# Turning the transformed SSM kernel with VectorE's 32x32 blocks instead of TensorE's transposes

## The chip, the cores and the metric

The kernel runs on one core of one Trainium2 chip. The metric is the device time of one execution, in microseconds (us), and the number shown is the median of several runs. Six things work side by side in a core: TensorE (PE in the profile, its weight loads PEld), VectorE (DVE), ScalarE (ACT), GpSimd (POOL), SyncE (SP, which here issues every transfer), and the 16 DMA engines that carry the transfers out. Each engine runs its own list of instructions in order and waits for others through semaphores.

## The reference

One block of a network: a modulated layer norm, a long causal convolution ("H3"), a gate, a second modulated layer norm and a SwiGLU feed-forward. All is float32, with 2048 positions, 512 channels and 1792 hidden units.

```python
mod = silu(c) @ w_mod                              # six vectors of 512: sa, ca, ga, sb, cb, gb
h  = layernorm(q) * (1 + ca) + sa
ks = sum_t k[s - t] * shift_k[:, t]                # 4 taps
kv = ks * v
y  = irfft(rfft(pad(kv)) * rfft(pad(ssm_k)))[:S] + kv * ssm_D
x  = q + ga * (h * y)
h2 = layernorm(x) * (1 + cb) + sb
out = x + gb * ((silu(h2 @ w_gate) * (h2 @ w_up)) @ w_down)
```

## The kernel before, in words

The kernel has two parts. The **front** makes `x`, normalizes it and forms the operands of the feed-forward. The **feed-forward** is a long row of 128x512 matmuls. It starts with the first product of the normalized input with gate and up weights (`gu_pe`, tile `g`).

**The convolution in the front.** The 512 channels are taken in four chunks of 128 (`c_` = 0 to 3). For each chunk the two sequences `kv` (called X) and `ssm_k` (called K) go through a two-step Fourier transform. They are multiplied point by point, and the product goes back through the inverse. For X the steps are:

- `tap0`, `tap`, `tms`, `tma`, `times_v`: the four taps and the product with v (ACT, DVE, POOL), with channels on the partitions.
- `x_turn`: TensorE transposes the chunk so that positions stand on the partitions (tile `kvt`), and ACT copies it out of PSUM.
- `x_first`: the first step of the transform, TensorE with the constant matrix `raw` (tile `er`) held and the data streamed. ACT copies the result (tile `s`) into `X[c_]`.
- `swap_x`: VectorE's transpose turns 32x32 blocks of `X[c_]` in place, four instructions for a chunk.
- `x3`: the second step (tile `px`, ACT copies it to `xs`), and `x_sum` (POOL or DVE) for the sum used by a three-multiplication complex product.

For K, before the change, the steps are:

- `k_first`: the first step, with the *data* (`SS[c_]`, tile `ss`) held and `raw` streamed. Channels then stand on the partitions. ACT copies the result in two halves into the tile `KT[c_]`.
- `k_turn`: TensorE transposes `KT[c_]`, 8 blocks of 128x128 at a time into one pair of PSUM banks (tile `kt`), and ACT (once DVE) copies the pair into `K[c_]`; four such steps for a chunk.

`KT` has one buffer for all four chunks (tag `f16`), and the last user of that buffer is the third piece of the modulation weights, `mod_load(2)`. Then `product3` forms the second step of K on TensorE (tile `pk`) and VectorE multiplies it with `xs`. `inv3` inverts the second step (tile `iv`), and ACT copies the result back into `X[c_]`. In `inv3s`, for the last chunk, VectorE turns it instead.

**Through memory and back.** Chunks 0, 1 and 2 then go out to device memory (`put`, one transfer of 2 MB, `away<-X`) and come back in another layout (`get`, four transfers of 512 KB, `X<-away`, pieces of 512 B). `y_pe` (tile `y`) is the last step of the inverse transform. It needs `X[c_]` back and the constant `einv` (tile `ei`). `y_into` and `y_gate` multiply `y` with the gate that `gate_n` (ACT) and `gate_p` (POOL or DVE) have made, and gather the statistics of the second layer norm. `rs1`, `rs2`, `rs3`, `norm1`, `norm_t`, `norm_s`, `hi1` and `lo1` make of them the first operands (`op`) of `gu_pe`.

**The order.** Nothing moves by itself: every instruction of an engine stands in program order, and the front is a list of calls written out by hand, one call a line. `e=act`, `e=dve` or `e=pool` says which engine does a step's vector work. A table `SLOTS` says which buffer each tile takes, so that a call may also wait for the last reader of a buffer. PSUM has four pairs of banks in the front (tag `ps`). SP issues all transfers in the order of the calls, and a transfer that must wait for a buffer holds up every transfer behind it.

## Time and profile before

| | |
|---|---|
| median of 3 runs | 574.13 us (574.13 to 574.15) |
| the profiled execution | 574.47 us, of which its span is 572.7 us |
| PE busy | 567.3 us, 99% of the span |
| DVE busy | 436.9 us, 76% |
| ACT busy | 301.0 us, 53% |
| POOL busy | 330.9 us, 58% |
| first `gu_pe` matmul | 152.09 us after the start of the span |
| granted TensorE clock | 1.00 |

The span runs from the first to the last instruction. The execution is 1.77 us longer than its span (574.47 - 572.7), and the profiled execution is 0.34 us above the median. Line 40 in the profile is the helper through which all engines record their instructions, so groups are told apart by their tiles: `kt<-ident,kt` are the transposes of `k_turn`, `kt<-s` the copies of `k_first`, `K<-kt` the copies of `k_turn`, `X<-X` the 32x32 turns of `swap_x`. A float32 matmul stands in the records as two instructions, a transpose as one.

### The profile page before, as it was taken

Reading aid. Unit: us, or ns where it says so; the run is one execution under the profiler, and the core shown is the slowest. Engines: PE = TensorE matmul, PEld = TensorE weight load, DVE = VectorE, ACT = ScalarE, POOL = GpSimd, SP = SyncE. Lnnn points to the kernel's source line nnn. Section 1 sums busy time; section 2 is a strip of 40 time slices with the busy share of each in tenths; the row PEclk is TensorE's granted clock in tenths of the full one; section 3 lists DMA queues with packets and bytes.
Section 4 is the critical chain, followed back from the end, with each engine's and each line's share of the span. In section 5 each row is a group of like instructions: output and inputs, shape, how many; then the busy total and the mean of one; then the engine's idle time right before and its main releaser. Section 6 shows DMA issues by size and latency. Waiting matters only on the chain.

```text
span 572.7 us, 10192 instructions
## 1 busy us (share of the span) xinstructions
PE 567.3 (99%) x4010; PEld 450.5 (79%) x4010; DVE 436.9 (76%) x625; ACT 301.0 (53%) x459; POOL 330.9 (58%) x303
## 2 busy tenths in 40 slices
PE   9999999999999999999999999999999999999997
PEld 9985476546888888888888888887888888888886
DVE  4897896989998866676576569857686868686766
ACT  3899989961754544434554556433434343434330
POOL 1348897789837866758979576452525252525210
PEclk9999999999999999999999999999999999999999
DMA  8976998997215364891899440354343434343403
GB/s 318 401 289 228 383 264 240 208 255 208 76 38 201 121 247 168 228 260 62 248 285 380 170 167 0 116 198 166 129 166 129 166 128 166 129 166 129 166 0 147
DMA packets 52545, 108.00 MB, mean 189 GB/s; under 512 B 19345, under 2 KB 34065, under 8 KB 46482
## 3 DMA queue, kind: packets, MB, share of 16 engines
q1 hardware_dynamic: 52498, 107.37, 55.9%
q8 instruction: 31, 0.51, 0.4%
q14 instruction: 16, 0.13, 0.1%
HBM read 72.74 MB, written 34.61 MB: 187 GB/s over the span
## 4 chain that ended last, share of the span: by engine, by line
PE 90%; DMA 3%; ACT 2%; DVE 2%; SPq 1%; issue 0%; POOL 0%; ACTq 0%; POOLq 0%
PE a L40 23%; PE dn L40 15%; PE c L40 12%; PE b L40 6%; PE da L40 6%; PE s L40 4%; PE g L40 4%; PE iv L40 3%; PE pk L40 3%; PE dc L40 3%; PE kvt L40 2%; DMA wm<-in_wmod 2%; PE kt L40 2%; PE px L40 2%; PE warm L40 1%; PE y L40 1%
## 5 line engine op out<-in xcount | busy, mean ns | idle before, releaser
L40 PE MATMUL a<-op,wsum 128*128 128x512 f32 x432 | 109.8, 390 | 0.0
L40 PEld LDWEIGHTS a<-op,wsum 128*128 128x128 f32 x432 | 81.0, 188 | 17.4 <-ACT p L40 0.4
L40 PE MATMUL dn<-wd,acts 128*128 128x512 f32 x336 | 84.8, 389 | 0.0
L40 PEld LDWEIGHTS dn<-wd,acts 128*128 128x128 f32 x336 | 63.1, 188 | 13.1
L40 ACT COPY p<-a 128x512 f32<-128x512 f32 x50 | 29.4, 587 | 57.7 <-PE a L40 57.7
L40 DVE TENSOR_TENSOR x<-x,dn 128x512 f32<-128x512 f32 (+1 forms) x65 | 43.2, 670 | 13.2 <-PE dn L40 12.9
L40 POOL TENSOR_TENSOR wa<-ws,wa 128x512 fp32r<-128x512 f32 (+1 forms) x28 | 32.0, 1165 | 26.2 <-ACT wa L40 26.2
L40 POOL TENSOR_TENSOR tb<-wds 128x256 f32<-128x256 f32 x12 | 8.9, 741 | 62.7 <-DVE wds L40 62.7
L40 ACT COPY r<-a 128x512 f32<-128x512 f32 x24 | 14.1, 587 | 53.8 <-PE a L40 53.8
L40 DVE TENSOR_TENSOR b<-r,c 128x512 f32<-128x512 f32 x24 | 16.7, 696 | 32.2 <-ACT sg L40 32.2
L40 POOL TENSOR_TENSOR wsum<-sr,wsum 128x512 fp32r<-128x512 f32 x28 | 40.1, 1456 | 0.0
L40 PE MATMUL c<-op,wsum 128*128 128x512 f32 x156 | 39.6, 389 | 0.0
L40 PE MATMUL c<-op,wa 128*128 128x512 f32 x156 | 39.6, 389 | 0.0
L40 PE MATMUL b<-op,wa 128*128 128x512 f32 x144 | 36.5, 389 | 0.0
L40 POOL TENSOR_TENSOR wd<-wds,wd 128x512 fp32r<-128x512 f32 x14 | 18.3, 1327 | 30.4 <-ACT wd L40 30.4
L40 PEld LDWEIGHTS c<-op,wa 128*128 128x128 f32 x156 | 29.3, 188 | 6.1
L40 PEld LDWEIGHTS c<-op,wsum 128*128 128x128 f32 x156 | 29.3, 188 | 6.1
L40 DVE TENSOR_TENSOR x<-x,da 128x512 f32<-128x512 f32 x48 | 32.7, 681 | 0.9 <-PE da L40 0.9
L40 DVE TENSOR_TENSOR xs<-pk,xs 128x1024 f32<-128x1024 f32 x24 | 27.6, 1213 | 7.3 <-PE pk L40 7.3
L40 PEld LDWEIGHTS b<-op,wa 128*128 128x128 f32 x144 | 27.0, 188 | 5.6
L40 POOL TENSOR_TENSOR s<-s,bcs 128x512 f32<-128x512 f32 x22 | 28.3, 1299 | 0.9
L40 ACT ACTIVATE sg<-a 128x512 f32<-128x512 f32 x26 | 15.5, 598 | 22.6 <-PE a L40 22.6
(200 smaller groups left out, 1352.2 us busy)
## 6 DMA issues: line engine op xcount, KB each, us to landing
ds<-wsum SPq DMA_DIRECT2D x12, 1024.0 KB, 7.6
wsum<-ds SPq DMA_DIRECT2D x12, 1024.0 KB, 6.4
dw<-wa SPq DMA_DIRECT2D x12, 768.0 KB, 5.9
wa<-dw SPq DMA_DIRECT2D x12, 768.0 KB, 4.3
ws<-in_wgu SPq DMA_DIRECT2D x16, 512.0 KB, 4.0
wds<-in_wdn SPq DMA_DIRECT2D x14, 512.0 KB, 4.8
...
```

The lines of the kernel that those rows point to most:

```text
L40: return lambda *a, **k: self.tc.keep_in_program_order(f(*a, **k))
```

## The change

K takes the way of X. `k_first` now holds `raw` and streams the data, so that its result has the layout of `x_first`'s and goes out of PSUM in one copy of 128x1024 for each step instead of two of 128x512. `k_turn` is gone. `k_swap` takes its place: four VectorE transposes in 32x32 blocks for each chunk, from `KT[c_]` into `K[c_]`. `x_first` is cut into four calls a chunk instead of two, with the same matmuls and copies. The list of the front is new throughout, and so are the buffer tables.

```diff
-    def x_first(c_, half, e=act):
-        if half == 0:
+    def x_first(c_, jq, e=act):
+        if c_ not in X:
             X[c_] = b16(f"X{c_}")
...
     def k_first(c_, jq, e=act):
         if c_ not in KT:
-            KT[c_] = f16(f"kt{c_}", (P, 4, 32, 32))
+            KT[c_] = f16(f"kt{c_}", (P, 32, P))
         ps = banks("s1")
         for jj in range(4):
             for a in range(2):
                 pe.matmul(
-                    ps[:, a, jj * P : (jj + 1) * P], SS[c_][rows(a), 4 * jq + jj], raw[rows(a), 4 * jq + jj],
+                    ps[:, a, jj * P : (jj + 1) * P], raw[rows(a), 4 * jq + jj], SS[c_][rows(a), 4 * jq + jj],
                     start=True, stop=True,
                 )
-        for a in range(2):
-            j = J * a + 4 * jq
-            copy(
-                e, KT[c_][:, :, j : j + 4, :].rearrange("p g j k -> p j g k"),
-                ps[:, a].rearrange("p (j g k) -> p j g k", j=4, g=4),
-            )
-
-    def k_turn(c_, m, e=act):
-        if m == 0:
+        copy(e, fours(KT[c_])[:, jq::4], ps.rearrange("p a (f d) -> p a d f", f=4))
+
+    def k_swap(c_, i):
+        if c_ not in K:
             K[c_] = b16(f"K{c_}")
-        ps = banks("kt").rearrange("p a (k d) -> p (a k) d", k=4)
-        src = KT[c_].rearrange("p g j k -> p (g j) k")
-        for k in range(8):
-            pe.transpose(ps[:, k], src[:, :, 8 * m + k], ident)
-        copy(e, fours(K[c_])[:, 2 * m : 2 * m + 2], ps.rearrange("p (g f) d -> p g d f", f=4))
+        r = slice(32 * i, 32 * i + 32)
+        dve.transpose(
+            fours(K[c_])[:, :, r].rearrange("p g d f -> p d g f"), fours(KT[c_])[:, :, r].rearrange("p g d f -> p d g f")
+        )
...
-    k_turn(3, 3, e=act)
...
+    product3(4, 0)
+    swap_x(14)
...
+    load_einv()
```

Several small steps change their engine in the new list. VectorE gives up one K copy, `mod_rep`, three `skip`, a `times_v`, an `x3` copy, `gate_n(2, 0)`, one of five `gate_p`, five of six `lo1`, two of four `add_y` and one of two `norm_s`. It takes one `x_first` copy and `wd_mul(0)`. POOL takes most of what VectorE gives up, and `mod_mul(0, 0)` from ACT. The feed-forward behind the front keeps its code.

VectorE's list at its start, from the first turns of chunk 0 to the products of chunk 0 (`K_308`, `K_320` are chunk 0's K, `u_300`, `u_296` the taps of chunk 2, `xs<-pk,xs` the products). Before:

```order
L40 STREAM_TRANSPOSE X_195<-X_195 128x32x8x4 x2
L40 COPY K_308<-kt 128x1024
L40 SCALAR_TENSOR_TENSOR u_300<-kt_245,sm,u_300 128x2047
L40 SCALAR_TENSOR_TENSOR u_300<-kt_245,sm,u_300 128x2046
L40 COPY crep<-csil 128x256
L40 SCALAR_TENSOR_TENSOR u_300<-kt_245,sm,u_300 128x2045
```

Now:

```order
L40 STREAM_TRANSPOSE X_196<-X_196 128x32x8x4 x4
L40 STREAM_TRANSPOSE K_320<-kt_248 128x32x8x4 x4
L40 SCALAR_TENSOR_TENSOR u_296<-kt_282,sm,u_296 128x2047
L40 SCALAR_TENSOR_TENSOR u_296<-kt_282,sm,u_296 128x2046
L40 SCALAR_TENSOR_TENSOR u_296<-kt_282,sm,u_296 128x2045
L40 TENSOR_TENSOR xs<-pk,xs 128x1024
```

All eight turns of chunk 0 now stand ahead of the taps of chunk 2, and the first product follows the taps at once.

SP's list from the first transfer out to memory to the last one back (`away` and `X<-away` are `put` and `get`, `x` the four loads of q, `ei` the constant for `y_pe`, `wm` modulation weights, `ws` gate and up weights). Before:

```order
L40 DMA x_718<-in_q 128x2048
L40 DMA ei<-in_e_inv 128x2048
L40 DMA away_786<-X_195 128x4096
L40 DMA x_788<-in_q 128x2048
L40 DMA x_790<-in_q 128x2048
L40 DMA X_195<-away_786 32x32x128 x4
L40 DMA away_1108<-X_400 128x4096
L40 DMA X_400<-away_1108 32x32x128 x4
L40 DMA ws<-in_wgu 128x1024
L40 DMA away_1498<-X_558 128x4096
L40 DMA wm<-in_wmod 128x2048
L40 DMA X_558<-away_1498 32x32x128 x4
```

Now:

```order
L40 DMA x_856<-in_q 128x2048
L40 DMA x_868<-in_q 128x2048
L40 DMA away_870<-X_196 128x4096
L40 DMA x_1091<-in_q 128x2048
L40 DMA X_196<-away_870 32x32x128 x4
L40 DMA away_1189<-X_410 128x4096
L40 DMA X_410<-away_1189 32x32x128 x4
L40 DMA ei<-in_e_inv 128x2048
L40 DMA away_1347<-X_547 128x4096
L40 DMA ws<-in_wgu 128x1024
L40 DMA wm<-in_wmod 128x2048 x2
L40 DMA X_547<-away_1347 32x32x128 x4
```

The constant `ei` has moved from ahead of the first `put` to behind the second `get`; two loads of q now stand ahead of the first `put`, and both halves of `wm` ahead of the last `get` instead of one on either side.

TensorE's list from the inverse of chunk 2 to that of chunk 3 (`y<-...` is `y_pe`). Before:

```order
L40 MATMUL iv<-xs,wc 64x512 x48
L40 MATMUL kt<-ident,kt_1293 128x128 x24
L40 MATMUL px<-X_1114,wc 32x512 x16
L40 MATMUL y<-X_195,ei 64x128 x8
L40 MATMUL y<-X_400,ei 64x128 x8
L40 MATMUL kt<-ident,kt_1293 128x128 x8
L40 MATMUL px<-X_1114,wc 32x512 x16
L40 MATMUL pk<-K_1475,wc 32x512 x48
```

Now:

```order
L40 MATMUL iv<-xs,wc 64x512 x48
L40 MATMUL px<-X_1024,wc 32x512 x8
L40 MATMUL y<-X_196,ei 64x128 x8
L40 MATMUL y<-X_410,ei 64x128 x8
L40 MATMUL px<-X_1024,wc 32x512 x8
L40 MATMUL warm<-ident 128x128 x5
L40 MATMUL px<-X_1024,wc 32x512 x16
L40 MATMUL pk<-K_1316,wc 32x512 x48
```

The transposes `kt` are gone, and the first `y_pe` stands ahead of three of the four `px` of chunk 3 instead of two.

More of the change, by code (lines that the diff above doesn't have):

```diff
@@ L282, in x_turn @@
         copy(e, x, pt)
[L284 to L287 removed]
+    def x_first(c_, jq, e=act):
+        if c_ not in X:
             X[c_] = b16(f"X{c_}")
[L289 to L304 removed]
+        x = XT[c_, jq // 2]
         ps = banks("s1")
@@ L1348, in adaln_h3_swiglu @@
-    product3(3, 2)
-    product3(3, 0)
-    product3(3, 1)
-    mod_mul(1, 1, e=act)
-    product3(2, 0)
-    product3(2, 2)
-    mod_part(1, 1, e=pool)
+    tap(3, 1)
+    product3(1, 2)
+    load_ssm(2)
+    x_sum(0, e=pool)
+    product3(0, 1)
+    tms(3, 2, e=act)
+    x_first(2, 0, e=act)
+    swap_x(7)
+    times_v(2, 2, e=pool)
+    x_first(2, 1, e=act)
+    product3(0, 0)
+    product3(0, 2)
+    mod_mul(0, 1, e=act)
+    swap_x(4)
+    k_swap(1, 0)
+    k_swap(1, 3)
+    k_swap(1, 1)
+    mod_part(0, 0, e=pool)
@@ new lines, in adaln_h3_swiglu @@
+    swap_x(5)
+    x_turn(2, 1, e=act)
+    tms(3, 3, e=act)
+    swap_x(6)
+    inv3(1, e=act)
+    tma(3, 2, 1, e=pool)
+    inv3(0, e=act)
+    x_first(2, 3, e=dve)
+    load_ssm(3)
+    k_swap(1, 2)
+    load_v(3)
+    x_first(2, 2, e=act)
+    swap_x(8)
+    swap_x(11)
+    swap_x(9)
+    do_stats(3, 0)
+    x3(2, 1, e=act)
+    tma(3, 2, 3, e=pool)
+    x3(3, 1, e=act)
+    x3(3, 2, e=act)
+    x_sum(3, e=dve)
+    product3(3, 0)
+    x3(2, 2, e=act)
+    skip(2, e=pool)
+    k_first(2, 0, e=act)
@@ new lines, in adaln_h3_swiglu @@
+    mod_part(0, 3, e=pool)
+    k_first(2, 1, e=act)
+    mod_mul(1, 0, e=act)
+    tma(3, 2, 2, e=pool)
+    x_sum(2, e=pool)
+    product3(2, 2)
+    room()
+    product3(3, 1)
+    product3(3, 2)
+    load_x(2)
+    product3(2, 0)
+    load_x(1)
+    put(0)
+    tma(3, 3, 2, e=pool)
+    x3(4, 2, e=act)
+    skip(3, e=pool)
+    tma(3, 3, 1, e=pool)
+    product3(2, 1)
+    times_v(3, 1, e=pool)
+    times_v(3, 3, e=pool)
+    times_v(3, 0, e=pool)
+    mod_mul(1, 1, e=act)
+    times_v(3, 2, e=pool)
@@ new lines, in adaln_h3_swiglu @@
+    inv3(3, e=act)
+    k_swap(2, 0)
+    inv3(2, e=act)
+    mod_part(1, 0, e=pool)
+    mod_part(1, 1, e=pool)
+    k_swap(2, 1)
+    mod_part(1, 2, e=pool)
+    k_swap(2, 2)
+    x_turn(3, 0, e=act)
+    mod_bc(0)
+    k_swap(2, 3)
+    x_turn(3, 1, e=act)
+    swap_x(10)
+    x3(4, 1, e=act)
+    mod_part(1, 3, e=pool)
+    k_first(3, 1, e=act)
+    x_first(3, 0, e=act)
+    x_first(3, 2, e=act)
+    x_sum(4, e=pool)
+    x_first(3, 1, e=act)
+    do_stats(1, 0)
+    mod_bc(1)
+    do_stats(3, 1)
@@ L1399, in adaln_h3_swiglu @@
+    gate_n(0, 1, e=act)
+    product3(5, 1)
+    load_einv()
     gate_p(0, 0, 1, e=pool)
-    load_w(1)
-    k_first(3, 3, e=act)
+    gate_p(0, 2, 1, e=pool)
+    product3(5, 2)
+    gate_n(2, 0, e=act)
     gate_n(3, 0, e=act)
-    swap_x(15)
-    swap_x(12)
-    gate_n(0, 1, e=act)
-    gate_p(0, 2, 1, e=pool)
+    inv3(4, e=act)
+    k_swap(3, 0)
+    k_swap(3, 3)
+    inv3(5, e=act)
+    put(2)
+    gate_p(3, 0, 1, e=dve)
+    x3(7, 1, e=act)
+    gate_p(0, 3, 1, e=pool)
+    y_pe(0, 0, 1)
@@ L1421, in adaln_h3_swiglu @@
[L1421 to L1442 removed]
+    y_into(0, 0, 1)
@@ L1452, in adaln_h3_swiglu @@
     inv3s(7)
     inv3s(6)
+    mod_row(2, 0)
+    mod_load(2, 1)
+    mod_row(2, 1)
     y_pe(2, 0, 1)
-    gate_p(2, 1, 1, e=pool)
-    gate_p(2, 3, 1, e=pool)
     y_gate(2, 0, 1)
-    y_pe(1, 0, 1)
-    gate_p(1, 2, 1, e=pool)
-    mod_row(2, 0)
+    mod_out(2, e=act)
+    get(2)
+    y_pe(0, 2)
+    y_pe(2, 2, 3)
+    y_into(0, 2)
+    y_pe(0, 3)
+    gate_p(1, 3, 1, e=pool)
     load_w(0)
-    y_pe(0, 3)
-    gate_p(3, 1, 1, e=pool)
+    w8_lo(1, e=pool)
     y_into(0, 3)
-    y_pe(0, 2)
@@ L1466, in adaln_h3_swiglu @@
-    mod_row(2, 1)
-    mod_out(2, e=act)
-    w8_lo(1, e=pool)
-    y_into(0, 2)
-    y_pe(2, 2, 3)
     rs1(0)
-    mod_T()
-    y_pe(1, 2, 3)
     rs2(0)
     rs3(0)
-    y_pe(3, 0, 1)
+    mod_T()
+    gate_p(1, 1, 1, e=dve)
+    y_gate(2, 2, 3)
+    load_wd(0)
     w8_hi(0)
```

440 lines of the change are left out of this document (178 added, 262 removed).

## The prediction

> **What bounds the kernel now.** I read the page first, then busy time by stretches, then the chain that ended last.
>
> ```profile
> span 572.7 us, 10192 instructions
> PE 567.3 (99%) x4010; PEld 450.5 (79%) x4010; DVE 436.9 (76%) x625; ACT 301.0 (53%) x459; POOL 330.9 (58%) x303
> ```
>
> TensorE is busy for 99% of the span, so work taken from it can shorten the kernel. The change touches only the front, which ends where the first feed-forward matmul `g` starts, at 152.09 us. Behind that point TensorE's work is unchanged, so I ask one thing only: by how much does `g` start earlier? I cut the front at the first data's arrival (4.86), at the end of chunk 2's products (107.62), at the end of the last turns (136.06), and at `g`:
>
> ```profile
> 4.86:107.62 102.76, 102.54 (x1486) 73.93 (x1490) 85.08 (x98) 91.96 (x123) 71.18 (x66) 1.00 0.91 301
> 107.62:136.06 28.44, 28.44 (x456) 15.73 (x440) 26.87 (x32) 15.54 (x18) 21.60 (x17) 1.00 0.92 244
> 136.06:152.09 16.03, 15.71 (x226) 13.54 (x218) 14.62 (x39) 8.94 (x12) 15.06 (x14) 1.00 0.36 113
> ```
>
> The columns are the length, then the busy time of PE, PEld, DVE, ACT and POOL, then the granted clock, the share of the DMA engines and GB/s. TensorE is full, but VectorE has only 17.7 us free in the first stretch (102.76 - 85.08) and 1.6 in the second. The transfers fill 0.91 and 0.92. Three resources lie close together, and the change lightens one of them. The chain shows how they meet at the end of the front:
>
> ```profile
> 104.86 5.35 PE iv L40 x88
> 110.23 1.94 ACT X L40 x2
> 112.19 6.98 DMA away<-X
> ...
> 126.34 12.29 DMA wm<-in_wmod
> ...
> 152.16 7.06 PE g L40 x30
> ```
>
> Chunk 2's inverse is copied out, goes to memory, comes back, and the last `wm` lands behind it at 138.63. So this end of the front hangs on two things: when chunk 2's products end, and what the transfers then need.
>
> **The change part by part.** *TensorE.* The removed transposes, and the two kinds of first-step matmul that change places:
>
> ```profile
> L40 PE MATMUL kt<-ident,kt 128*128 128x128 f32 x128 | 16.8, 282 | 0.2 <-ACT kt L40 0.2
> L40 PE MATMUL s<-x,er 64*128 64x128 f32 x256 | 15.9, 275 | 0.0
> L40 PE MATMUL s<-er,ss 64*128 64x128 f32 x256 | 15.7, 275 | 0.0
> ```
>
> On the chain 16 transposes take
>
> ```profile
> 37.73 1.99 PE kt L40 x16
> 83.64 1.80 PE kt L40 x16
> ```
>
> that is 0.113 to 0.124 us each, so 128 take 14.4 to 15.9; I take 15.9. Holding `raw` instead of the data costs nothing: X's matmuls of that form (15.9) take what K's took (15.7). TensorE's own floor for the kernel is thus 574.13 - 15.9 = 558.2. The Trainium skill (TensorE: Matmul & The Clock Gate, Part 4: PE-mode transpose) gives about 275 ns for such a transpose inside a kernel. By that the removal would be worth an estimated 128 x 0.275 = 35 us. The row's duration of 282 ns agrees with the page, but the chain shows that transposes overlap, so the duration isn't the price.
>
> *ScalarE and VectorE.*
>
> ```profile
> L40 ACT COPY K<-kt 128x1024 f32<-128x1024 f32 x15 | 15.7, 1094 | 0.7 <-PE kt L40 0.7
> L40 ACT COPY kt<-s 128x512 f32<-128x512 f32 x32 | 16.9, 691 | 0.3 <-PE s L40 0.2
> L40 ACT COPY X<-s 128x1024 f32<-128x1024 f32 x16 | 16.1, 1110 | 0.1
> L40 DVE STREAM_TRANSPOSE X<-X 128x1024 f32<-128x1024 f32 x16 | 19.1, 1218 | 1.5 <-ACT X L40 1.5
> L40 DVE STREAM_TRANSPOSE X<-iv 128x1024 f32<-128x1024 f32 x4 | 7.5, 2084 | 0.0
> L40 DVE COPY K<-kt 128x1024 f32<-128x1024 f32 x1 | 1.2, 1225 | 1.7 <-PE kt L40 1.7
> L40 DVE COPY xs<-px 128x1024 f32<-128x1024 f32 x1 | 1.2, 1225 | 2.3 <-PE px L40 2.3
> L40 DVE TENSOR_TENSOR ss<-ss,bcs 1x128 f32<-1x128 f32 x3 | 2.0, 651 | 0.0
> ```
>
> ScalarE loses 15.7 + 16.9 and gets back 16.1 for the 16 full copies. It gets 16.5 us lighter and bounds nothing. VectorE gets sixteen `k_swap`. One costs between 1.19 us (19.1/16, the turn of X) and 1.88 (7.5/4, the turn out of PSUM into another layout). The form is that of X's turn, from SBUF to SBUF with the same pattern, so I take 1.19: 19.1 us in all, up to 30.1 at the other end. Ahead of the end of chunk 2's products stand twelve of them (14.3 us) and one `x_first` copy (1.2). One turn of X (1.2) has moved behind that point. Gone are the two copies (2.4), the three `skip` (2.0), and two steps that the timeline shows:
>
> ```profile
> 38.62 0.74 DVE L40 TENSOR_TENSOR vt<-u,vt 128x512 f32<-128x512 f32 x1
> 94.09 0.99 DVE L40 TENSOR_SCALAR s<-x,rsa 128x512 f32<-128x512 f32 x2
> 100.74 6.88 DVE L40 TENSOR_TENSOR xs<-pk,xs 128x1024 f32<-128x1024 f32 x6 [3.38 <-PE pk L40]
> 139.76 0.68 DVE L40 TENSOR_TENSOR y<-y,s 128x512 f32<-128x512 f32 x1
> ```
>
> VectorE's work from 4.86 to the end of these products (now 100.74 + 6.88 = 107.62) becomes 85.1 + 14.3 + 1.2 - 1.2 - 2.4 - 2.0 - 0.7 - 1.0 = 93.3. Its floor for that point is 4.86 + 93.3 = 98.2, which is 9.4 earlier than now. TensorE's floor there, without the 96 transposes of chunks 0 to 2 (96 x 0.124 = 11.9 us), is 95.7. So **VectorE takes TensorE's place as the bound of the front**, and 9.4 is the most that it leaves. How much of the 9.4 comes depends on VectorE's remaining waits. Now it waits 17.7 us there, mostly for these:
>
> ```profile
> DVE xs L40 <- PE pk L40: 7.3, 3, 3.6
> DVE x L40 <- PE kvt L40: 2.5, 2, 1.6
> DVE xs L40 <- PE px L40: 2.3, 1, 2.3
> DVE K L40 <- PE kt L40: 1.7, 1, 1.7
> ```
>
> (total, times, longest). The waits of the two copies (2.3 and 1.7) go with them. The waits for `kvt` (2.5) and for the first data (1.0, the rest of the start) stay, since TensorE's first 15 us are the same. Of the other 10.2 us (7.3 of them for `pk`) I keep a quarter, 2.3, because TensorE now has 2.5 us less to do than VectorE up to that point (95.7 against 98.2). That gives 5.8 us of waits and an end of chunk 2's products at 104.0, which is 3.6 earlier. Both ends stay for the range: no waits but the start's 3.5 (101.7, 5.9 earlier) and all of today's but the copies' (111.9, 4.3 later).
>
> What the other engines take over has room. POOL is busy for 71.2 + 21.6 = 92.8 of the 131.2 us from 4.86 to 136.06. It gets some ten instructions more there, about 13 us at the 1.3 us of its commonest ones:
>
> ```profile
> L40 POOL TENSOR_TENSOR s<-s,bcs 128x512 f32<-128x512 f32 x22 | 28.3, 1299 | 0.9
> ```
>
> If that cover were gone, the first `y_into`, which waits for POOL's four `gate_p` of row block 0, would hold all products of chunk 3 behind it on VectorE.
>
> *The transfers behind chunk 2.* SP now sends `put(2)`, one `ws`, both `wm`, then `get(2)`. Plain loads ran at 388 GB/s, and the 512-byte pieces of `get` at about 210:
>
> ```profile
> 20.00:30.00 10.00, 9.78 (x115) 9.47 (x112) 8.26 (x7) 9.75 (x14) 5.91 (x5) 1.00 0.99 388
> 95.00:100.00 5.00, 5.00 (x96) 3.90 (x88) 2.36 (x3) 5.00 (x10) 2.85 (x4) 1.00 0.38 117
> 110.00:112.00 2.00, 2.00 (x23) 1.28 (x12) 1.97 (x3) 1.77 (x2) 0.48 (x1) 1.00 0.08 21
> 128.00:131.00 3.00, 3.00 (x60) 1.28 (x48) 3.00 (x3) 0.00 (x0) 2.85 (x3) 1.00 1.21 210
> ```
>
> `wm` needs the buffer of `KT`, which is free once the last `k_swap` has run. That is some 8 us behind chunk 2's products on VectorE, so before `put(2)` has landed, and the wait costs nothing unless VectorE is held up there. The sum: `put(2)` starts at 112.19 - 3.6 = 108.6, lands 6.98 later at 115.6, 0.5 + 2.1 MB at 388 take 6.8 (122.4), and the 2.1 MB of `get` at 210 take 10.0 (132.4). Now the chain has `wm` as the last to land; then it is `get(2)`, and three `y_pe` wait for it with 32 matmuls, two groups of this size:
>
> ```profile
> 136.38 1.97 PE L40 MATMUL y<-X,ei 128*64 128x128 f32 x32
> 152.09 7.13 PE L40 MATMUL g<-op,wg 128*128 128x512 f32 x30
> ```
>
> That is 3.9 us (136.3). From the last `y_into` of row block 0 (139.76) to `g` (152.09) it is 12.3 us now, through statistics, norm, transposes and splitting, the same steps as then. So `g` starts at 148.6, **3.5 us earlier**. The profiled execution would go from 574.47 to 571.0. It stands 0.34 above the median, so the median goes from 574.13 to **570.6**.
>
> **The rivals.**
>
> *VectorE and the transfers hide all but the start's waits.* For it speaks that nearly everything VectorE waits for comes from TensorE, which gets 15.9 us lighter. Against it speaks that the steps of one chunk depend on each other across three engines. With 2.0 us of waits chunk 2's products end at 100.2, 7.4 earlier. The same transfers and the same tail follow, and the time is 574.13 - 7.3 = 566.8. Even here TensorE's 15.9 are out of reach.
>
> *The waits stay as they are.* VectorE gets its turns, but waits 9 us or so in all, for PSUM pairs and for ScalarE's copies. Chunk 2's products then end near 107.6 and the time stays within 1.1 us of 574.1. For it speaks the order in which all eight turns of chunk 0 and three taps of chunk 2 stand on VectorE ahead of the first product, while TensorE's list has `pk` waiting for that product's PSUM pair.
>
> *The transfers come too late, and the kernel gets slower.* Two loads of q now stand ahead of the first `put`, one behind it, and `ei` behind the second `get`. So 4.2 MB of plain loads lie between vt's last load and `put(2)`, where 2.1 MB follow `put(0)` now. The other 2.1 MB cost 2.1/0.388 = 5.4 us. Free time of the DMA engines there is 3.1 us in 95 to 100 and 1.8 us in 110 to 112. The first is the turnaround between a `put` that lands and its `get`. SP's list has nothing to fill it with, since `ei` stands behind the `get`. Only 1.8 us are filled, and `put(2)` starts at 112.19 + 5.4 - 1.8 = 115.8 whatever VectorE has done. `ei` is late as well. The first `y_pe` waits for it on TensorE with three `px` and all `pk` of chunk 3 behind. With the same tail `g` starts 7.2 us later than forecast, at 155.8, and the time is 574.13 + 3.7 = 577.8. It decides from the point where chunk 1's `get` and `ei` land after 108.6; beyond 112.2 the kernel loses. Against it speaks that the three loads of q wait for buffers only, and may go early enough.
>
> *TensorE goes cold in its new waits.* The clock was 1.00 throughout, but TensorE also had no wait over 1.34 us. What a cold start costs, the first and second batch of `warm` show:
>
> ```profile
> 1.34 6.48 PE L40 MATMUL warm<-ident 128*128 128x128 f32 x32 [1.34 <-POOL ident masks.py:199]
> 23.12 1.38 PE L40 MATMUL warm<-ident 128*128 128x128 f32 x10
> ```
>
> 32 records would take 4.4 us at the second rate (0.138 each) and took 6.5, so 2.1 are lost. If the waits for `ei` and for `get(2)` each cause such a start, the forecast becomes 570.6 + 4.2 = 574.8, and a third one makes it 576.9, slower. The Trainium skill (TensorE: Matmul & The Clock Gate, Why this matters for your kernels) warns of idle gaps over about 3 us, behind which the array runs at half clock again. No run here shows such a gap yet.
>
> **How the numbers follow.** The forecast has 0.40, with its own range 568.1 to 572.9 (1.2 to 6 us faster). The fuller hiding has 0.20, no change 0.15, the late transfers 0.20, and three cold starts 0.05. The likeliest is the forecast: 570.6. For 8 times in 10 the range goes to 565.0 on the one side, beyond the second case's 566.8, and to 577.0 on the other, short of the third's 577.8, so that about 0.07 and 0.13 stay outside. A dearer `k_swap` (11 us on VectorE at 1.88) would also end beyond the upper end. Changes under 0.2% (1.15 us) can't be told from none: faster 0.40 + 0.20 = 0.60, same 0.15, slower 0.20 + 0.05 = 0.25.
>
> **What would show it.** TensorE's span share falls below 99%, by waits before `pk`, before the first `y` and before the `y` of chunk 2. `K<-kt` on VectorE has 16 rows near 1.19 us. VectorE is busy for over 90% from 4.86 to the end of the last turns, and chunk 2's products end near 104. `put(2)` starts near 108.6, the last thing to land ahead of `g` is `X<-away`, and `g` starts near 148.6. From `g` to the end it stays 420.6 us (572.7 - 152.1). The prediction is wrong if that last stretch grows (POOL late with the next weights), if `ei` lands after 108.6, if `k_swap` costs much over 1.2 us, or if the clock falls below 1.00.

## The result, and the profile after

The changed kernel takes 586.95 us (median of 4 runs, 586.70 to 587.41), against 574.14 us for the kernel before beside it. The ratio is 1.0223, with a 95% interval of 1.0205 to 1.0240: **slower by 12.8 us**. I had forecast 570.6.

The page of the changed kernel, to be read against the one before (span 572.7, PE 567.3 at 99%, clock full throughout):

```profile
span 584.9 us, 9904 instructions
PE 561.4 (96%) x3882; PEld 436.7 (75%) x3882; DVE 453.1 (77%) x624; ACT 286.9 (49%) x428; POOL 360.2 (62%) x319
PEclk9997999989998999999999999999999999999999
```

TensorE does 128 instructions less and is busy for only 5.9 us less. Its clock now dips twice in the front, and once behind `g` (175 to 190 us). POOL has 29.3 us more. Busy time by stretches, cut as in the prediction at the end of chunk 2's products, at the end of the last turns, and at `g`:

```profile
4.86:107.82 102.96, 95.13 (x1380) 60.70 (x1386) 94.38 (x101) 77.76 (x90) 84.26 (x73) 0.97 0.81 281
107.82:141.92 34.10, 28.00 (x440) 14.64 (x426) 28.40 (x30) 16.57 (x20) 25.28 (x20) 0.90 1.08 292
141.92:157.15 15.23, 14.22 (x214) 13.22 (x211) 14.92 (x37) 7.38 (x11) 13.95 (x12) 1.00 0.19 59
```

The first stretch is 102.96 us long, as long as before (102.76), with 7.4 us less of TensorE's busy time. The second grew from 28.44 to 34.10. So `g` starts at 157.15 instead of 152.09. From `g` to the first `dn` it is 26.5 us (157.15 to 183.61), against 21.0 before (152.09 to 173.09). That makes 5.06 + 5.46 of the 12.2 us of span. The other 1.7 lie right behind the first `dn`, as TensorE's rows show, in the changed kernel and in the one before:

```profile
183.61 2.54 PE L40 MATMUL dn<-wd,acts 128*128 128x512 f32 x6 [1.88 <-DVE wd L40]
173.09 1.52 PE L40 MATMUL dn<-wd,acts 128*128 128x512 f32 x6
```

TensorE waited 1.88 us ahead of it, and its granted clock was 0.58 from 183.61 to 186.15. These six took 1.02 us longer than before, and the twelve `g` behind them 0.73 (3.61 against 2.88). The chain that ended last, with columns start, length, engine, tile:

```profile
30.78 2.89 POOL wm L40
34.36 7.90 POOL wm L40 x3
42.25 2.04 POOL vt L40
...
89.79 12.29 DMA away<-X
103.97 11.83 DMA X<-away
115.80 2.44 issue
118.24 3.68 PE y L40 x32
...
134.41 7.04 DVE X L40 x4
...
164.19 2.35 DVE s L40 x2
166.54 4.46 DVE x L40 x2
```

Before, TensorE had 90% of this chain; now it has 75%. The chain passes through POOL's multiplication of `wm`, through `put(1)`, `get(1)` and another 2.44 us (in which, as the run with `ei` earlier will show, TensorE waits for `ei`) to the first `y`, and from 132 us up to `g` almost only through VectorE. TensorE's two longest waits stand in its own list (the bracket gives the idle time ahead of a group and what ended it):

```profile
45.38 2.33 PE L40 MATMUL kvt<-ident,vt 128*128 128x128 f32 x8 [4.78 <-POOL vt L40]
118.24 3.68 PE L40 MATMUL y<-X,ei 128*64 128x128 f32 x32 [6.10 <-issue]
```

### The profile page after: what moved, and what is told of

Read it like the earlier page. It is cut to its first block, busy times and chain, and to the rows that moved or that the text cites. A ratio compares the mean times of both kernels' runs of the same rounds, so it can differ in the third digit from the quotient of the medians.

```text
span 584.9 us, 9904 instructions
## 1 busy us (share of the span) xinstructions
PE 561.4 (96%) x3882; PEld 436.7 (75%) x3882; DVE 453.1 (77%) x624; ACT 286.9 (49%) x428; POOL 360.2 (62%) x319
## 4 chain that ended last, share of the span: by engine, by line
PE 75%; DVE 11%; DMA 4%; ACT 4%; POOL 3%; issue 2%; SPq 0%; DVEq 0%; ACTq 0%; POOLq 0%
PE a L40 22%; PE dn L40 15%; PE c L40 12%; PE b L40 6%; PE da L40 6%; PE dc L40 3%; PE pk L40 2%; DMA away<-X 2%; DMA X<-away 2%; POOL wm L40 2%; PE iv L40 2%; DVE x L40 2%; DVE X L40 2%; PE kvt L40 2%; DVE s L40 1%
## 5 line engine op out<-in xcount | busy, mean ns | idle before, releaser
L40 PEld LDWEIGHTS c<-op,wsum 128*128 128x128 f32 x156 | 29.3, 188 | 6.1
L40 PEld LDWEIGHTS c<-op,wa 128*128 128x128 f32 x156 | 29.3, 188 | 6.1
L40 POOL TENSOR_TENSOR s<-s,bcs 128x512 f32<-128x512 f32 x24 | 31.1, 1311 | 0.9
L40 PE MATMUL pk<-K,wc 64*32 64x512 f32 x384 | 25.1, 630 | 2.7 <-DVE xs L40 2.7
```

The source lines that it names most:

```text
L40: return lambda *a, **k: self.tc.keep_in_program_order(f(*a, **k))
```

## The experiments

Each time stands beside runs of the kernel before on the same chip. The runs of one kernel lie up to 3.6 us from their median, so I read differences between two variants from the intervals of their ratios.

### Order and turns apart

The change has two parts, so two orders with and without VectorE's turns give four kernels. The first run has the new `k_first` and `k_swap` in the old order, one `k_swap` at each of the 16 places of `k_turn`:

```diff
-            KT[c_] = f16(f"kt{c_}", (P, 4, 32, 32))
+            KT[c_] = f16(f"kt{c_}", (P, 32, P))
...
-    k_turn(0, 0, e=act)
-    k_turn(0, 1, e=dve)
+    k_swap(0, 2)
+    k_swap(0, 3)
```

> The order of the kernel before, with only the way K is transformed exchanged: the DFT matrix is stationary, and each of the 16 TensorE turns is replaced, at its place, by one VectorE turn. Theory O (the new order loses the time; turning K on VectorE costs no more than the 1.2 us per turn that was seen, and TensorE is relieved): 566 to 574 us, clearly below the changed kernel's 587. Rival V (VectorE as the bound of the front loses the time, whatever the order): 580 us or more.

It took 588.98 us, ratio 1.0259 (1.0233 to 1.0284). My theory fell at once: VectorE's turns alone, in the old order, cost as much as the whole change. The rows show where. VectorE's list in this run:

```profile
24.86 2.32 DVE L40 STREAM_TRANSPOSE K<-kt 128x1024 f32<-128x1024 f32 x2
...
37.91 2.37 DVE L40 STREAM_TRANSPOSE K<-kt 128x1024 f32<-128x1024 f32 x2 [3.30 <-ACT kt L40]
40.21 2.31 DVE L40 SCALAR_TENSOR_TENSOR u<-kt,sm,u 128x2045 f32<-128x2045 f32 x1
```

The last tap `u` of chunk 2 comes behind the turns: it starts at 40.21 and ends at 42.5, where before it ended at 35.2. Ahead of it stand six turns (7.05 us) and, in the second row, a wait of 3.30 us for ScalarE's copies of K. These copies waited in turn: at 32.29 ScalarE stood 2.27 us for VectorE's turns of chunk 0, because this order has one buffer for the copy (`KT`). So part of the cost here is that buffer's, not the turns'. POOL's `vt` waits for the tap, TensorE's `kvt` for `vt`. POOL and TensorE in this run:

```profile
42.65 5.07 POOL L40 TENSOR_TENSOR vt<-u,vt 128x512 f32<-128x512 f32 x3 [12.45 <-issue]
44.89 2.34 PE L40 MATMUL kvt<-ident,vt 128*128 128x128 f32 x8 [7.62 <-POOL vt L40]
123.99 0.34 SPq L40 DMA_DIRECT2D away<-X  x1
```

The third row is `put(2)` in SP's list, 11.8 us later than before (112.19). A single turn costs what I forecast; the price lies in what it delays on other engines.

The next run leaves all 16 turns out, so that only TensorE's and ScalarE's relief is left:

```diff
-            KT[c_] = f16(f"kt{c_}", (P, 32, P))
+            K[c_] = (f16 if c_ == 2 else b16)(f"K{c_}", (P, 32, P))
...
-    k_swap(0, 2)
-    k_swap(0, 3)
```

> The run with the old order and VectorE's turns (589 us), now without any turn of K: ScalarE copies the transformed K straight into the buffers that the products read, and the 16 VectorE turns are left out (so the products use K unturned, and the output is not the reference's). Theory V (VectorE's 16 turns, 18.9 us in its rows, are what costs; without them the removal of TensorE's 128 transposes is a gain): 558 to 570 us, chunk 2's products end at 98 to 104 instead of 118. Rival W (the time goes in the waits between the engines or in TensorE's slower clock behind them, and comes back whatever VectorE does): above 574, chunk 2's products end later than 107.6.

It took 572.40 us, ratio 0.9967 (0.9951 to 0.9983), a gain of 1.9 us by the ratio. Neither theory had that. Without any turn, the removal of 128 transposes and 32.6 us of ScalarE's copies, with 16 copies put in, is worth 1.9 us, not the 15.9 of TensorE's time. Its first stretch, up to the end of chunk 2's products:

```profile
4.86:106.40 101.54, 94.46 (x1392) 64.68 (x1394) 85.38 (x97) 82.57 (x97) 74.80 (x66) 0.97 0.91 303
```

It is 1.2 us shorter than before. TensorE is now idle for 7.1 us of it and VectorE, with as much work as before (85.4 against 85.1), still waits for 16.2. So most of the 17.7 us that I had read as VectorE waiting for a full TensorE don't come from TensorE's load. The run isn't a clean price of the relief, though. VectorE's taps started earlier, POOL's four `vt` beside them took 7.00 us instead of 4.99, and TensorE waited for them:

```profile
30.04 1.97 PE L40 MATMUL kvt<-ident,vt 128*128 128x128 f32 x8 [3.32 <-POOL vt L40]
```

Its granted clock was 0.50 from 30 to 34. So 1.9 us is what this order gains from the relief; that no other order would gain more isn't shown. The turns then cost (1.0259 - 0.9967) x 574.1 = 16.8 us in this order.

The new order without turns completes the four:

```diff
-            KT[c_] = f16(f"kt{c_}", (P, 32, P))
+            K[c_] = (f16 if c_ in (1, 3) else b16)(f"K{c_}", (P, 32, P))
...
-    k_swap(0, 0)
-    k_swap(0, 3)
```

> The changed kernel without any turn of K (ScalarE copies the transformed K straight into the buffers that the products read; the output is not the reference's). With the old order this took the time from 589 to 572. Theory V (the turns' 18.6 us on VectorE cost, in either order): 568 to 575. Rival O (the new order, with its work on POOL, its late loads and its tail, loses most of the time by itself): 578 or more.

It took 585.18 us, ratio 1.0187 (1.0157 to 1.0218). The rival holds. In the new order the turns cost (1.0223 - 1.0187) x 574.1 = 2.1 us, hardly more than the intervals leave open: the order hides them, or its own waits do. But the order by itself, with the engines that it gives the steps to, is (1.0187 - 0.9967) x 574.1 = 12.6 us slower than the old one, though both have the same work left out.

| | VectorE turns | no turns |
|---|---|---|
| old order | 589.0 | 572.4 |
| new order | 587.0 (the change) | 585.2 |

### What holds the time when TensorE is relieved

Two runs start from the old order without turns (572.4) and take POOL's adds of `wm` (six `mod_part`, twelve adds), or VectorE's statistics of q, out as well.

```diff
-    mod_part(0, 0, e=pool)
...
-    mod_part(0, 1, e=pool)
-    mod_part(0, 2, e=pool)
```

> The old order without turns of K (572.4 us), and POOL's twelve adds of wm left out in addition (15 us of POOL's work between 59 and 87 us; the output is not the reference's). The question is what holds this kernel at 572 when TensorE has lost 128 transposes and VectorE has no turn in their place. Theory Q (POOL's unbroken work from 51 to 104 us sets the pace): 564 to 569. Rival (VectorE or the transfers set it): 571 or more.

It took 570.32 us, ratio 0.9931 (0.9907 to 0.9955).

```diff
-        for i in rows_:
+        if name[0] == "a" and 0 in rows_:
+            dve.memset(mv, 1.0)
+        for i in rows_ if name[0] != "a" else ():
```

> The old order without turns of K (572.4 us), and VectorE's statistics of q left out in addition (16 pairs, 13.4 us of VectorE's work between 75 and 91 us, replaced by four memsets; the output is not the reference's). Theory V2 (VectorE set the pace of the front already in the kernel before, though TensorE was busy for 99%): 560 to 568. Rival (POOL or the transfers set it): 571 or more.

It took 570.77 us, ratio 0.9945 (0.9926 to 0.9964). The theories of a full POOL or a full VectorE asked for 3.4 and 4.4 us or more (569 and 568 us at most), their rivals for less than 1.4 (571 or more). The first got about 2; the second about 1, which the intervals hardly tell from nothing. Neither time lies clearly with one theory. `put(2)` moved from 110.91 to 106.81 and 108.52, `g` from 150.4 to 147.4 and 148.0. Taking 13 to 15 us from POOL or VectorE alone frees 2 to 3 us ahead of `g`. So none of the three engines TensorE, POOL and VectorE sets the pace alone. Transfers and ScalarE weren't tested in this way.

### The new order's waits, one at a time

The first run takes POOL's long multiplication away:

```diff
-    mod_mul(0, 0, e=pool)
+    mod_mul(0, 0, e=act)
```

> The changed kernel with the first four multiplications of wm by csil on ScalarE instead of POOL. Theory O1 (POOL's 11.5 us for them hold vt, and through it the transposes of chunk 2 on TensorE, which then sits idle for 4.8 us): that idle time goes, put(0) starts 3 to 5 us earlier and the time falls to 582 to 585. Rival (VectorE's own work is the bound there, and the idle time only moves): 586 to 588, and put(0) starts within 1 us of 72.2.

It took 586.21 us, ratio 1.0207 (1.0169 to 1.0245): not told from the change. `put(0)` did start 5 us earlier (67.12 instead of 72.15) and TensorE's wait for `kvt` went. What came in its place, in VectorE's, POOL's and TensorE's lists of this run:

```profile
65.65 6.75 DVE L40 TENSOR_TENSOR xs<-xs 128x512 f32<-128x512 f32 x2
67.29 1.27 POOL L40 TENSOR_TENSOR u<-u,tm 128x512 f32<-128x512 f32 x1
68.94 1.25 POOL L40 TENSOR_TENSOR u<-u,tm 128x512 f32<-128x512 f32 x1
70.27 5.73 POOL L40 TENSOR_TENSOR vt<-u,vt 128x512 f32<-128x512 f32 x4
73.79 3.50 PE L40 MATMUL pk<-K,wc 64*32 64x512 f32 x32 [5.27 <-DVE xs L40]
140.94 5.38 PE L40 MATMUL y<-X,ei 128*64 128x128 f32 x64 [4.22 <-issue]
```

Two adds of VectorE that take 0.7 us each when POOL is quiet took 6.75 here, the first 5.10 (65.65 to 70.75) and the second 1.74, beside a POOL that paused only at 70.2. TensorE waited 5.3 us behind them and then ran `pk` in 3.50 instead of 1.95. At the end, the `y` of chunk 2 waited for `get(2)`, which nothing had brought forward.

The second run loads `ei` earlier:

```diff
     put(1)
+    load_einv()
     get(1)
...
-    load_einv()
```

> The changed kernel with the load of ei issued between put(1) and get(1) instead of behind get(1). Theory O2 (the first y matmuls wait 6.1 us for ei, and px and pk of chunk 3 stand behind them): the wait goes, VectorE's last turns out of PSUM end 3 to 6 us earlier than 141.9, and the time falls to 581 to 584. Rival (these y matmuls would wait for X of chunk 1, which get(1) brings later still, or the stall moves to get(2)): 586 to 588.

It took 586.33 us, ratio 1.0218 (1.0171 to 1.0265). The wait for `ei` went, with 1.15 us for `get(1)` left in its place, and chunk 3's turns ended at 136.6, 5.3 earlier, as the theory said. But `g` started at 157.5. The rival had it: the stall moved to `get(2)`.

```profile
140.22 5.38 PE L40 MATMUL y<-X,ei 128*64 128x128 f32 x64 [4.16 <-issue]
```

The third run has the old end of the front, from the last inverse on, with those gates in it that the new order has still to do there. Three of the steps that moved, `...` marking what is left out between:

```diff
     inv3s(6)
...
+    gate_p(3, 2, 1, e=pool)
...
+    wd_mul(0, e=pool)
...
-    gate_p(3, 2, 1, e=dve)
...
-    add_y(2, 0, 4, (0, 1), e=pool)
...
-    wd_mul(0, e=dve)
...
+    add_y(2, 0, 4, (0, 1), e=dve)
```

> The changed kernel up to the last inverse transform, and from there the order and engines of the kernel before (gates of rows on POOL, sums of x and y on VectorE, subtractions of op mostly on VectorE, wd multiplied early on POOL). Theory O3 (POOL and VectorE hold each other up when both read two SBUF operands at once, and this costs the 5.4 us between the first g and the first dn): g to the first dn takes 21 to 22 us instead of 26.5, and the time falls to 581 to 583. Rival (the stretch is long only because its inputs come late from the front): it stays at 25 us or more, and the time at 585 to 588.

It took 588.17 us, ratio 1.0242 (1.0221 to 1.0263). TensorE's list:

```profile
158.31 0.47 PE L40 MATMUL nt<-ident,n 128*128 128x128 f32 x1 [5.54 <-ACT n L40]
166.89 7.10 PE L40 MATMUL g<-op,wg 128*128 128x512 f32 x30
187.83 1.52 PE L40 MATMUL dn<-wd,acts 128*128 128x512 f32 x6
```

From `g` to `dn` it took 20.9 us, as the theory said, and from `g` to the end 420.5, against 420.6 in the kernel before. But POOL still had 14 of its gate instructions to do (135.52 to 153.66) and came to the variance at 156.1; ScalarE's norm waited 10.0 us for it and TensorE 5.5. `g` started 9.7 us later. The wait moved to the other side of `g`.

### Two prices measured at the head

Ahead of the first data POOL and VectorE are idle, so extra instructions there show a price by itself. The times of these two kernels (590.59 and 609.54 us, one run each) aren't the question. The first of two runs asks what a multiplication by a column costs on POOL.

```diff
+    for _ in range(2):
+        pool.tensor_scalar(du[:, 0], du[:, 0], mhalf[:, 0:1], None, op0=ALU.mult)
+        pool.tensor_scalar(du[:, 0], du[:, 0], -0.5, None, op0=ALU.mult)
+        pool.tensor_tensor(du[:, 0], du[:, 0], du[:, 1], op=ALU.mult)
```

> The changed kernel with six extra POOL instructions at its head, on a buffer of their own, while POOL has nothing else to do until 11 us: multiplication of 128x512 by a column, by a constant, and by a second operand, once before VectorE's first work and once during VectorE's taps. Theory A (multiplying by a column is dear on POOL by itself): the first one takes 2.3 us or more with VectorE idle. Theory B (it is as cheap as the other forms, about 1.3 us, and took 2.9 because VectorE's taps held the way to SBUF): 0.7 to 1.4 us with VectorE idle, and over 2 only during the taps.

```profile
2.33 1.58 POOL L40 TENSOR_SCALAR du<-du,mhalf 128x512 f32<-128x512 f32 x1 [1.04 <-DVE du L40]
3.99 1.50 POOL L40 TENSOR_SCALAR du<-du 128x512 f32<-128x512 f32 x1
5.58 1.27 POOL L40 TENSOR_TENSOR du<-du 128x512 f32<-128x512 f32 x1
6.95 1.88 POOL L40 TENSOR_SCALAR du<-du,mhalf 128x512 f32<-128x512 f32 x1
```

It costs 1.58 us with VectorE idle and 1.88 beside VectorE's short taps, so neither theory is right. In its place in the changed kernel it took 11.49/4 = 2.87. There the four took 3.60, 2.71, 2.70 and 2.52 us, beside VectorE's long taps. Two of these taps took 2.66 us each, and 2.35 in the run with `wm` on ScalarE, so each slows the other. That the taps are the whole of the difference isn't shown.

The second sets VectorE and POOL against each other.

```diff
+    for _ in range(7):
+        dve.tensor_tensor(dd[:, 0], dd[:, 0], dd[:, 1], op=ALU.mult)
+    for _ in range(12):
+        pool.tensor_tensor(du[:, 1], du[:, 1], du[:, 1], op=ALU.mult)
+    for _ in range(6):
+        dve.transpose(dw, dv)
```

> The changed kernel with extra instructions at its head, ahead of the first data, on buffers of their own: four two-operand multiplications 128x512 on VectorE alone, three on POOL alone, then eight on VectorE and twelve on POOL at once, and six 128x1024 turns on VectorE while POOL's go on. Theory P (two-operand instructions of VectorE out of SBUF and POOL's can't run at once): VectorE's rise from 0.67 us to 1.3 to 2 us each, or wait for the whole of POOL's row; the turns, with one operand, stay at 1.2. Rival (the two run side by side): 0.67 and 1.27 us each throughout.

```profile
4.29 2.08 DVE L40 TENSOR_TENSOR dd<-dd 128x512 f32<-128x512 f32 x3
11.89 10.08 DVE L40 TENSOR_TENSOR dd<-dd 128x512 f32<-128x512 f32 x7
21.89 7.63 DVE L40 STREAM_TRANSPOSE dw<-dv 128x1024 f32<-128x1024 f32 x6
7.18 20.15 POOL L40 TENSOR_TENSOR du<-du 128x512 f32<-128x512 f32 x15 [5.89 <-DVE du L40]
```

Theory P holds. VectorE's multiplication takes 2.08/3 = 0.69 us alone and 10.08/7 = 1.44 beside POOL. POOL's row mixes cases: one instruction took 1.26 alone, 1.37 beside VectorE's multiplications and 1.04 beside the turns. The turns, with one operand, take 1.23 to 1.25 beside POOL. The Trainium skill (SBUF — State Buffer, Who interferes with whom) says that a VectorE instruction with two SBUF inputs contends with a GpSimd instruction that reads SBUF. The same page of the Trainium skill (Summary: rules for kernel authors) says that the second to issue is blocked until the first finishes. The trace agrees that they hold each other up. That each waits for the whole of the other it doesn't show: 1.44 us for one is less than 0.69 + 1.04. In the run with `wm` on ScalarE the add that took 5.10 us ran beside four POOL instructions that followed each other without a gap, and ended 0.5 us behind the first pause in POOL's list (0.08 us at 70.2). At the head POOL pauses as long between any two. That the add needs such a pause is inferred.

### Repairs together

Single repairs move waits. The next runs put them together. First `wm` and `ei`:

```diff
-    mod_mul(0, 0, e=pool)
+    mod_mul(0, 0, e=act)
...
     put(1)
+    load_einv()
...
-    load_einv()
```

> The changed kernel with two repairs at once: wm multiplied on ScalarE and ei loaded ahead of get(1). Each alone moved the time by under 1 us. Theory S (waits stand side by side: behind ei the next one is chunk 2's way through memory, which starts when VectorE has ended chunk 2's products, and neither repair touches that): g still starts within 1.5 us of 157.2 and the time is 584 to 587. Rival (the two repairs work on different stretches and add up): g at 153 or earlier and 581 or less.

It took 586.97 us, ratio 1.0227 (1.0199 to 1.0254), with `g` at 155.6, at the edge of theory S. The two don't add up to a gain in the time.

Then VectorE's sum of `xs` was moved to POOL, on top of the multiplication on ScalarE:

```diff
-    x_sum(3, e=dve)
+    x_sum(3, e=pool)
```

> The run with wm multiplied on ScalarE, and in addition the sum of xs for product 3 on POOL instead of VectorE, where its two adds took 6.75 us (65.65 to 72.40) instead of 1.4 while POOL ran without a gap. Theory P (VectorE's two-operand adds out of SBUF wait for POOL's instructions, which also read SBUF): VectorE loses the 5 us of waiting, TensorE's idle time of 5.3 us before pk goes, chunk 2's products end 3 to 5 us earlier than 107.3 and put(2) starts at 108 to 110; the time itself then falls by 1 to 4 us, to 582 to 585. Rival (the adds were waiting for their input from ScalarE, not for POOL): put(2) stays at 112 to 113 and the time at 586 or more.

It took 593.46 us, ratio 1.0332 (1.0313 to 1.0352), within the rival's range (586 or more), but with `put(2)` at 117.54, later than either theory had it. POOL's list is full there, and the sum came late:

```profile
  POOL xs L40: 13.4, 3
```

That is the idle time of VectorE ahead of the products, ended by POOL's `xs`. All repairs on top of this run did not mend that:

```diff
     put(1)
+    load_einv()
...
-    mod_load(2, 0)
     inv3s(7)
     inv3s(6)
-    mod_row(2, 0)
+    get(2)
+    mod_load(2, 0)
     mod_load(2, 1)
...
     lo1("B21", 1, e=pool)
+    wd_mul(0, e=pool)
...
-    add_y(2, 0, 4, (0, 1), e=pool)
+    add_y(2, 0, 4, (0, 1), e=dve)
     norm_s(1, 2, e=dve)
-    wd_mul(0, e=dve)
```

> All repairs together on the changed kernel: wm multiplied and the sum of xs moved as in the run above, ei loaded ahead of get(1), get(2) issued ahead of both wm loads (TensorE's rows for wm then behind the y of chunk 2), and at the end of the front one row gate moved from VectorE to POOL, the sums of x and y all on VectorE and wd multiplied on POOL. Theory (several waits stand side by side at the end of the front, chunk 3's products behind ei and chunk 2's way through memory, so that only removing all of them shows): g starts at 148 to 152, g to the first dn takes 21 to 24 us, and the time is 568 to 577. Rival (VectorE's total work in the front bounds it, and each repair only moves a wait): g at 156 or later and 583 or more.

It took 592.18 us, ratio 1.0309 (1.0290 to 1.0328). `put(2)` was at 117.2 already, so the run says nothing on the repairs behind it. The next run goes back to the one with `wm` and `ei`, has the same repairs at the end without the moved sum, and gives two gates to POOL in its idle time:

```diff
-    mod_load(2, 0)
     inv3s(7)
     inv3s(6)
-    mod_row(2, 0)
+    get(2)
+    mod_load(2, 0)
...
     w8_lo(1, e=pool)
+    gate_p(1, 1, 1, e=pool)
+    gate_p(3, 2, 1, e=pool)
...
-    gate_p(1, 1, 1, e=dve)
...
-    gate_p(3, 2, 1, e=dve)
+    wd_mul(0, e=pool)
...
-    add_y(2, 0, 4, (0, 1), e=pool)
+    add_y(2, 0, 4, (0, 1), e=dve)
```

> The run above, and in addition get(2) issued ahead of both wm loads, TensorE's rows for wm behind one y, two row gates moved from VectorE to POOL where POOL sits idle for 6 us, wd multiplied on POOL, and the sums of x and y all on VectorE. Theory S: with get(2) landing at 132 to 136 instead of 141, g starts at 149 to 153, g to the first dn takes 22 to 24 us, and the time is 573 to 579. Rival (VectorE or POOL are full up to g, and the wait moves again): g at 156 or later and 583 or more.

It took 582.84 us, ratio 1.0148 (1.0120 to 1.0176). That is faster than the change by (1.0223 - 1.0148) x 574.1 = 4.3 us. In the profiled execution the gain lies between `g` and `dn` (24.0 us instead of 26.5) and behind `dn`; `g` itself was at 158.5, as the rival had it. `get(2)` came earlier, but now the `wm` behind it was last, and TensorE's rows for `wm` stood ahead of `y`. From the chain:

```profile
128.98 11.20 DMA wm<-in_wmod
140.22 1.96 PE mr L40 x16
```

The transfers that follow chunk 2 end near 140 us in either order: with `wm` first `get(2)` was last, here `wm`. The next run lets VectorE's sum read one operand from PSUM:

```diff
-            e.tensor_tensor(t[:, a], xs[n, 1][:, a], xs[n, 2][:, a], op=ALU.add)
+            e.tensor_tensor(t[:, a], xs[n, 1][:, a], (xs[n, 2] if e is pool else xs[n, 2, "ps"])[:, a], op=ALU.add)
```

> The run above, and in addition VectorE's sum of xs for product 3 reads one of its two operands from PSUM instead of SBUF. Theory P (the 6.75 us of these two adds were waiting for POOL, which shares the way to SBUF with two-operand instructions of VectorE, as the run at the head showed with 1.44 us against 0.69): they take 1.4 us, TensorE's wait of 5.3 us before pk goes, put(2) starts 3 to 5 us earlier and the time falls by 2 to 5 us against the run above, to 569 to 576, which would be at or under the kernel before. Rival (their input from ScalarE was late, or VectorE's later work fills what they leave): put(2) within 1 us of the run above, and the same time.

```profile
65.57 1.25 DVE L40 TENSOR_TENSOR xs<-xs,px 128x512 f32<-128x512 f32 x2
162.76 6.81 DVE L40 TENSOR_TENSOR x<-x,s 128x1024 f32<-128x1024 f32 x3
```

The two adds took 1.25 us instead of 6.75, and `put(2)` started at 110.80, 3.1 earlier than in the run above: theory P on both counts, with the same POOL beside it. The time was 583.36 us, ratio 1.0156 (1.0137 to 1.0176), no better. Of 3.1 us at `put(2)` only 0.9 were left at `g` (157.6). Nor is the repair free: TensorE waited 3.09 us for the PSUM that the sum now holds, and 4.36 for `get(1)`. The last row shows the same contention behind `g`: three sums of x and y took 6.81 us, where before four took 5.3.

The last two runs mend TensorE's list at the two waits that this trace shows. The first of them also changed POOL's list:

```diff
-    y_pe(0, 0, 1)
     swap_x(12)
...
     x3(6, 1, e=act)
+    y_pe(0, 0, 1)
     k_swap(3, 2)
...
-    mod_row(2, 0)
-    mod_row(2, 1)
-    mod_out(2, e=act)
-    y_pe(0, 2)
...
     y_into(0, 3)
+    y_pe(0, 2)
...
+    mod_row(2, 0)
+    mod_row(2, 1)
...
     rs3(0)
+    w8_lo(1, e=pool)
+    gate_p(1, 1, 1, e=pool)
+    gate_p(3, 2, 1, e=pool)
```

> The run before (583 us), with TensorE's list mended at two places where that run's trace shows it waiting: the matmuls for wm stand behind the y of row block 0 instead of ahead of them (there they held y for wm until 138.8), and three px of chunk 3 stand ahead of the first y (which waited 4.4 us for get(1)); POOL's root of the variance is ahead of its last weights and gates. Theory S (TensorE's order of waiting is what is left): chunk 3's turns end 2 to 4 us earlier, g starts at 151 to 154 and the time is 576 to 580. Rival F (VectorE, POOL and the transfers are all full up to g, so that no order of TensorE gains): g at 156 or later, 582 to 585. In neither case does the kernel come under the 574 of the kernel before.

It took 586.62 us, ratio 1.0230 (1.0211 to 1.0249), with `g` at 160.7: later than both theories. POOL sat idle for 7.6 us ahead of the variance and then held VectorE's `y` of row block 1: a wait of my own making. Without that placement:

```diff
     load_w(0)
+    w8_lo(1, e=pool)
+    gate_p(1, 1, 1, e=pool)
+    gate_p(3, 2, 1, e=pool)
     y_into(0, 3)
...
     rs3(0)
-    w8_lo(1, e=pool)
-    gate_p(1, 1, 1, e=pool)
-    gate_p(3, 2, 1, e=pool)
```

> The run before (586.6 us), with POOL's last weights and two gates put back ahead of the root of the variance: behind it, they left POOL idle for 7.6 us and came late for y of row block 1 (VectorE waited 2.7 us, ScalarE's norm 2.7). Theory S: chunk 3's turns still end near 136.4, g starts at 152 to 156 and the time is 577 to 581. Rival F (all three resources are full up to g): g at 157 or later, 582 or more. In both cases it stays above the 574 of the kernel before.

It took 582.47 us, ratio 1.0143 (1.0126 to 1.0160). TensorE's waits went, chunk 3's turns ended at 136.3, and `g` started at 156.6, between the two expectations and nearer to the rival. VectorE then waited 2.0 us for `pm` and 2.3 for the next `y`. Together the repairs take 4.6 us of the 12.8 off. No version came under the kernel before, and none of the runs points to one that would.

## Why the prediction was wrong

**"TensorE is full, so work taken from it can shorten the kernel": this step failed first.** It read a busy share of 99% as the bound. The run without turns has all of TensorE's relief and nothing on VectorE in its place, and gains 1.9 us of 15.9, less than the 3.5 that I forecast with all the turns on VectorE. My quoted rows name only the last link of VectorE's waits, `pk` on TensorE. The runs' rows show what stands ahead of it: taps, `vt`, `kvt` and `xs`, in which TensorE is one link of several.

**"VectorE takes TensorE's place as the bound", floor 98.2, 5.8 us of waits: the work was right, the waits weren't.** VectorE's work up to the end of chunk 2's products is 94.38 us (forecast 93.3), and a turn costs what I took:

```profile
L40 DVE STREAM_TRANSPOSE K<-kt 128x1024 f32<-128x1024 f32 x16 | 18.6, 1206 | 0.0
```

But the waits are 102.96 - 94.38 = 8.6, so the products end at 107.82, not 104.0. The largest of them stands behind `kvt`, `vt` and POOL's `wm`:

```profile
49.70 1.23 DVE L40 TENSOR_TENSOR xs<-pk,xs 128x1024 f32<-128x1024 f32 x1 [5.49 <-PE pk L40]
```

This was the term on which the whole gain of 3.5 us rested. I had kept a quarter of the waits because TensorE has less to do (a quarter of 10.2 is 2.6, too, not the 2.3 that I added). As most of the waits weren't TensorE's, that had little ground. My rival of unchanged waits (within 1.1 us of 574.1) was nearer up to this point; the one in which the waits are hidden still better was further off.

**"POOL has room", ten more instructions at 1.3 us: mis-sized, and asked in the wrong way.** The four multiplications took 11.49 us, not 5.2. More than the price, it matters what was queued behind them: `vt`, with TensorE's `kvt` behind it (4.78 us idle). And POOL's load isn't free of VectorE's. A sum over busy shares can't see that the two hold each other up.

**`put(2)` to `get(2)`, 23.8 us: mis-sized.** `put(2)` started at 113.11, not 108.6. `get(2)` was sent out at 123.01 to 132.5, behind both `wm`. With `ei` out of the way, TensorE got it at 140.2, 26.6 us behind `put(2)` (113.60). In the changed kernel itself the wait for `ei` hides it: its `y` at 139.38 don't wait.

**The rival "transfers come too late" was right about `ei`.** The first `y` waited 6.1 us for it, with `px` and `pk` of chunk 3 behind. It forecast `g` at 155.8, and `g` came at 157.15. That is partly luck: it had the transfers hold `put(2)` until 115.8, and `put(2)` started at 113.11, right behind chunk 2's inverse. With `ei` early, `g` didn't move, so this wait alone doesn't set it either.

**The rival "TensorE goes cold" was right about the clock, not about the places.** The granted clock was 0.79 and 0.87 in the 20 us around that wait:

```profile
110.00:120.00 10.00, 3.90 (x57) 2.15 (x43) 7.74 (x7) 3.87 (x5) 6.77 (x5) 0.79 1.09 347
120.00:130.00 10.00, 10.00 (x149) 4.96 (x153) 6.58 (x13) 5.31 (x7) 4.83 (x4) 0.87 1.05 348
```

32 `y` matmuls took 3.68 us instead of 1.97, and the `px` behind them 0.33 longer, so this start cost 2.0 us (forecast 2.1). It was the one for `ei`; that for `get(2)` didn't come. Two others did. Behind the 4.78 us ahead of `kvt` the clock was 0.50 from 45 to 50, where `kvt` took 2.33 us instead of 1.17 and `pk` 3.53 instead of 1.95. Behind the 1.88 us ahead of `dn` it was 0.58. Whether the first two lengthen the kernel isn't shown; the third is the 1.7 us behind `dn`. By the Trainium skill's rule (TensorE: Matmul & The Clock Gate, Why this matters for your kernels), cited there, gaps over about 3 us do this. The trace agrees for the gaps of 4.78 and 6.10, and shows a loss behind shorter ones too: that of 1.88, and one of 2.38 in the run with `wm` on ScalarE, where the clock fell to 0.50 and 32 `y` matmuls took 3.26 us:

```profile
114.05 3.26 PE L40 MATMUL y<-X,ei 128*64 128x128 f32 x32 [2.38 <-ACT xs L40]
```

**"From `g` to the end it stays 420.6 us": failed by 7.1 us.** Of these 5.46 lie between `g` and `dn` and 1.7 are the clock's behind `dn`. I had left the end of the list, with its moved `add_y`, `gate_p`, `lo1` and `wd_mul`, at nothing. There VectorE and POOL both work on two operands out of SBUF:

```profile
160.19 3.87 DVE L40 TENSOR_TENSOR s<-s,bcs 128x512 f32<-128x512 f32 x4
166.46 4.54 DVE L40 TENSOR_TENSOR x<-x,s 128x1024 f32<-128x1024 f32 x2
163.47 2.85 POOL L40 TENSOR_TENSOR x<-x,s 128x1024 f32<-128x1024 f32 x1
166.62 3.29 POOL L40 TENSOR_TENSOR x<-x,s 128x1024 f32<-128x1024 f32 x1 [0.31 <-DVE s L40]
```

Of VectorE's two sums the first took 1.21 us and the second, beside POOL's of 3.29, 3.41; before they took 1.2 to 1.7. The run with the old end gave 20.9 us from `g` to `dn`, so the new end is what stretched it; that contention is the whole of it is argued, not shown, as that run also changed the order.

**What stays open.** The repairs take 4.6 of the 12.8 us back; why the new order costs the rest isn't shown. The order and the engines that it gives the steps to were never parted. The runs show only that waits of VectorE, POOL, the transfers and TensorE lie close together: of 3.1 to 5.3 us removed at one place, at most 0.9 was left at `g`.
